# A fused attention and expert kernel: the first batch's turned z gets the layout of the later ones

## The chip, the cores and the metric

The kernel runs on one core of one Trainium2 chip. Its time is the device time of one execution in microseconds (us). The core has four compute engines that the text names: TensorE (PE in the rows; its weight loads are PEld), VectorE (DVE), ScalarE (ACT) and GpSimd (POOL). SyncE (SP) and GpSimd issue the DMAs. Each engine works through its own instructions in order; semaphores tie the engines together.

## The reference

Two layers follow each other. The first is an attention without softmax over 8 batches of 2816 tokens, with keys and queries both z (64 wide) and values v (256 wide):

```
scores = z @ z.T / 2816
attn   = relu(scores) ** 2
x      = u * (attn @ v)
```

The second is a mixture of experts on all 22528 rows of x: a dense part, relu(x @ w1_dense) @ w2_dense, plus, for the one of 8 experts that has the largest logit of x @ w_gate, the softmax weight of that expert times relu(x @ w1[e]) @ w2[e].

## The kernel before, in words

A batch is cut into 22 blocks of 128 tokens. z is turned so that its 64 columns lie on partitions; as they fill only half of the 128, two copies are kept, one on partitions 0 to 63 and one on 64 to 127, and TensorE runs two 64-row matmuls beside each other, one on either half. For the batches after the first the turn is a DMA transpose (`turn_z`, line 127), which takes two blocks at a time and so leaves block k on the lower half and block k + 1 on the upper; `cross_z` (line 136) then copies the blocks to the other half, crossed, into the odd places. For the first batch, whose z comes in three DMAs, TensorE makes the turn itself (`turn_z0`, line 227): each block is turned twice, once into either half, in four parts, and every part is copied out of PSUM by ScalarE or VectorE (line 233). The function `swapped` tells by batch which layout holds.

The scores are symmetric: a block of A = relu(.)**2 for queries i and keys k is the transpose of that for queries k and keys i. So groups of 2, 4, 4, 4, 4 and 4 query blocks (`groups`) compute only the key rows that no earlier group has; `far_steps` brings the others by DMA transposes on SP's queue (line 557), into spare places of the weight tile or of the tile `zn` (`slots`, `mirror`). `scores` (line 466) makes a tile s of 1024 columns in one of four pairs of PSUM banks (`pairs`); `relu` takes it to SBUF (`first`, lines 482 and 484) and squares it into A (`second`, lines 498 and 500). `av` runs the output matmuls of two query blocks at a time (line 698): 22 key blocks with each half of the array on one of the two outputs, then, after a change of rows, 22 more with the halves exchanged. At the change (`swap_rows`), TensorE must not have the two halves write the same output; so either one touch (`touch`, line 635, a matmul into a PSUM pair of its own) and two tiles of scores stand between (a filled change), or two touches (a plain change, also used where the logits of the expert stage have to go in).

The order of all this is made at build time by a planner written in Python. `now` is its clock of TensorE, `free` its clocks of the other engines. Work for ScalarE, VectorE and GpSimd is put in a list with `offer(ready, rank, ways, then)`, where `ways` gives for each engine a planned duration; `best` takes what can start earliest, the lower rank first among equals, and refuses an engine that would end later than another one would, by more than a margin:

```
                if len(ways) > 1:
                    end = min(at[x] + ways[x][0] for x in ways if x != eng)
                    if t + dur > end + (0.0 if rank in (0.9, 4) else 0.6):
                        continue
```

`fill` places scores between output matmuls while PSUM pairs are free by these clocks; `need` lets the planner's TensorE wait for blocks of A. `at` and `soon` tie further work to ticks, two for every pair of query blocks: `small_constants` (from line 257) writes, at tick 7 and in one piece, eight small tables that the routing of the expert stage uses much later, without the planner's clock of VectorE being moved.

After the attention, from about 540 us, the expert stage runs: for each tile of tokens two matmul layers of the dense part and of one expert (lines 1107 and 1118), with ScalarE and VectorE taking the results out and GpSimd scattering the rows to the output.

Of the kernel before, what the change touches and what calls it, by code (L numbers as in the profile page):

```python
# [12 lines left out]
ALU = mybir.AluOpType  # L13
AX = mybir.AxisListType
ET = mybir.EngineType
P = 128
# [3 lines left out]
def kernel(  # L20
# [12 lines left out]
    nc = tc.nc  # L33
# [6 lines left out]
    nK = S // P  # L40
# [79 lines left out]
    def swapped(b, x):  # L120
        return x % 2 if b else 0
# [10 lines left out]
    def cross_z(b, h):  # L132

        x = zT_of[b][:].rearrange("p (k h) t -> p k h t", h=2)
        mine, other = slice(h * dq, (h + 1) * dq), slice((1 - h) * dq, (2 - h) * dq)
        nc.vector.tensor_copy(x[mine, :, 1, :], x[other, :, 0, :])
        if h == 1:
            z_there.add(b)
# [76 lines left out]
    parts0 = [(0, Z1), (Z1, Z2), (Z2, 16), (16, nK)]  # L215
    z0_cast = [0.25, 1.7, 2.5, 2.5]
    z0_left = list(range(len(parts0)))
    z0_turned = {}

    def turn_z0(n):  # L220
        k0, k1 = parts0[n]
        until(lambda: pairs[0][0] if pairs else None)
        x = take_pair()
        zp = banks(x, "zp", (P, 2, 8, P), BF)[:, 0]
        for k in range(k0, k1):
            for h in range(2):
                nc.tensor.transpose(out=zp[h * dq:(h + 1) * dq, k - k0, :],
                                    in_=z_of[0][:, k, :], identity=ident[:])
        now[0] = max(now[0], z0_cast[n]) + 0.05 + 0.13 * (k1 - k0)
        c = (k1 - k0) * P  # L230

        def copy(eng):
            (nc.scalar.copy if eng == "act" else nc.vector.tensor_copy)(
                zT_of[0][:, k0:k1, :], zp[:, :k1 - k0, :])

        def there(t):
            z0_turned[n] = t + 0.15
            give_pair(t + 0.1, x)

        offer(now[0] + 0.2, -1, {"act": (0.2 + c / 1280, copy), "dve": (0.16 + c / 1960, copy)}, there)  # L240

    te = const.tile([P, E], I32, name="te")
# [5 lines left out]
    free.update(act=1.0, dve=0.3, pool=2.4)  # L248
# [7 lines left out]
    def small_constants():  # L256
        nc.vector.memset(wg[:, 0, 0:1], 0.0)
        nc.gpsimd.dma_start(out=wg[:], in_=moe_w_gate.rearrange("(c p) e -> p c e", p=P))
        nc.gpsimd.affine_select(out=ntri[:], in_=ntri[:], compare_op=ALU.is_ge,
                                fill=0.0, base=0, pattern=[[-1, P]],  # L260
                                channel_multiplier=1)
        nc.vector.tensor_copy(desc8[:], ti[:])
        nc.vector.tensor_copy(ecap[:], te[:])
        nc.vector.tensor_copy(base[:], te[:])
        nc.vector.tensor_copy(sf[:], it[:])
        nc.vector.tensor_scalar(out=it0[:], in0=sf[:, 0:NH], scalar1=float(P), scalar2=None,
                                op0=ALU.mult)
        nc.vector.tensor_scalar(out=it1[:], in0=sf[:], scalar1=float(T2), scalar2=float(T2 - 1),
                                op0=ALU.mult, op1=ALU.add)
        nc.vector.tensor_copy(pjf[:], pj[:])  # L270
        nc.vector.memset(one8[:], 1.0)
# [44 lines left out]
    def best():  # L316
        pick = None
        for op in todo:
            rank, num, ready, ways, then = op
            at = {x: max(free[x], ready) for x in ways}  # L320
            if "pool" in ways:

                at["pool"] = max(at["pool"], both["dve"])
            for eng, (dur, fn) in ways.items():
                t = at[eng]
                if len(ways) > 1:

                    end = min(at[x] + ways[x][0] for x in ways if x != eng)
                    if t + dur > end + (0.0 if rank in (0.9, 4) else 0.6):
                        continue  # L330
                if rank == 1:
                    if not r_free:
                        continue
                    t = max(t, r_free[0])
                key = (t, rank, num)
                if pick is None or key < pick[0]:
                    pick = (key, op, eng)
        return pick
# [39 lines left out]
    def slots(b):  # L378

        return (list(mirror) if b < B - 1 else []) + ([(1, 5)] if 0 < b < B - 1 else [])  # L380
# [68 lines left out]
    def scores(n, ks, x=None):  # L449
# [5 lines left out]
        if n == 0:  # L455
# [3 lines left out]
            until(lambda: max(z0_turned[x] for x in mine) if set(mine) <= set(z0_turned) else None)  # L459
            until(lambda: pairs[0][0] if pairs else None)  # L460
        sx = take_pair() if x is None else x
        s = banks(sx, "s")
        for y, k in enumerate(ks):
            for h in range(2):
                r = slice(h * dq, (h + 1) * dq)
                nc.tensor.matmul(out=s[:, h, y * c:(y + 1) * c],  # L466
                                 lhsT=zT[r, k + h - swapped(b, h), :],
# [3 lines left out]
        relu(n, ks, s, c, now[0] + (0.3 if n == 0 else 0.2), sx)  # L471
        run(now[0])

    def relu(n, ks, s, c, ready, sx):
# [36 lines left out]
        def half(t):  # L511
            give_pair(t + 0.1, sx)
            more = 0.08 if n < 3 else 0.0
            ways = {"act": (0.12 + more + c / 600, second), "dve": (0.08 + more + c / 480, second)}
            if n < 3:

                ways = {"act": (0.2 + c / 600, second), "pool": (0.15 + c / 290, second)}
            offer(t + 0.15, 4 if n > 2 else 0.9, ways, done)

        more = 0.06 if n < 3 else 0.0  # L520
# [18 lines left out]
    def block(n, k, c):  # L539

        b, _, w = groups[n]
        for a in far[n]:
            _, j0, wj = groups[a]
            if j0 <= k < j0 + wj:
                x = c * wj + (k - j0 ^ swapped(b, c))
                return turned_to(a, n, w)[:, x * P:(x + 1) * P]
        c ^= swapped(b, k)
# [91 lines left out]
    def swap_rows(n):  # L639

        keep[0] = 0
        if at_swap or ahead(n) is None or n == 0 and not (len(pairs) > 1 and pairs[1][0] <= now[0]):
# [576 lines left out]
    at(7, small_constants)  # L1219
# [203 lines left out]
```

## Time and profile before

| | us |
|---|---|
| median of 3 runs | 861.49 (860.99 to 862.01) |
| the profiled execution | 861.74 |
| its span, first to last instruction | 860.0 |

| engine | busy us | share of the span |
|---|---|---|
| TensorE | 847.5 | 99% |
| TensorE weight loads | 760.5 | 88% |
| ScalarE | 686.9 | 80% |
| VectorE | 643.0 | 75% |
| GpSimd | 495.3 | 58% |

In the table a share is busy time over the whole span; in the attention stage ScalarE and VectorE are fuller than in the expert stage. A matmul's busy time includes its way through the array, which overlaps the next one's, so TensorE's pace is read from the starts of its instructions rather than from their lengths. In rows of a timeline the first number is the start, the second the time from the first start to the last end of the merged instructions, "x8" their count, and in square brackets stands the idle time of the engine before them and what ended it.

### The profile page before, as it was taken

The numbers are of one execution on the slowest core, as the hardware profiler recorded it, in microseconds if no ns is written. First come the engines' busy times: TensorE is split into PE (matmuls) and PEld (weight loads), VectorE is DVE, ScalarE is ACT, GpSimd is POOL, SyncE is SP. The second block draws the span as 40 slices with busy tenths as digits, with TensorE's granted clock in tenths as the row PEclk, the third lists the DMA queues.
The fourth block names the chain that finished last, engine by engine and source line by source line (L and its number), as shares of the span: only waits on it lengthen the run. The fifth ranks groups of instructions, "written<-read, shape, count | busy, mean of one in ns | idle before, by whom it ended". The sixth has DMA issues, their size and how long they took to land. (4 is left out here: it accounts for less than half of the span.)

```text
span 860.0 us, 30273 instructions
## 1 busy us (share of the span) xinstructions
PE 847.5 (99%) x12238; PEld 760.5 (88%) x12238; DVE 643.0 (75%) x1096; ACT 686.9 (80%) x857; POOL 495.3 (58%) x612
## 2 busy tenths in 40 slices
PE   8999999999999999999999999999999999999997
PEld 7998898898898899899899888888888888889996
DVE  6999978988988988988988994756554444445664
ACT  8999978977987987987987994677777777777775
POOL 6404456357346557446546567777767655555565
PEclk9999999999999999999999999999999999999999
DMA  7989999999999989989999787765544544444332
GB/s 161 179 173 175 188 164 182 219 169 185 207 179 191 209 176 193 208 178 178 199 190 173 143 167 126 123 139 133 132 113 125 121 118 114 114 109 103 92 97 87
DMA packets 279086, 134.00 MB, mean 156 GB/s; under 512 B 247710, under 2 KB 255006, under 8 KB 278944
## 3 DMA queue, kind: packets, MB, share of 16 engines
q1 hardware_dynamic: 252240, 76.42, 51.5%
q0 software_dynamic: 26704, 55.64, 30.0%
q8 instruction: 96, 1.57, 0.8%
q14 instruction: 46, 0.38, 0.2%
HBM read 61.53 MB, written 37.03 MB: 115 GB/s over the span
## 5 line engine op out<-in xcount | busy, mean ns | idle before, releaser
L698 PE MATMUL o<-vb,A 64*128 64x256 bf16 x6992 | 444.2, 269 | 0.0
L698 PEld LDWEIGHTS <-A 64*128 64x128 bf16 x6992 | 371.4, 94 | 32.1 <-issue 0.7
L868 POOL DMA_INDIRECT xs<-pays,pi x176 | 188.9, 1074 | 167.9 <-issue 60.3
L482 ACT ACTIVATE r<-s 128x1024 f32<-128x1024 f32 (+1 forms) x230 | 227.4, 1007 | 41.6 <-PE s L466 22.7
L1112 ACT ACTIVATE ring<-h_ps 128x1024 bf16<-128x1024 f32 x180 | 183.1, 1018 | 87.7 <-PE h_ps L1107 85.6
L498 ACT ACTIVATE A<-r 128x1024 bf16<-128x1024 f32 (+1 forms) x246 | 247.0, 1031 | 2.2 <-DVE r L484 0.9
L484 DVE TENSOR_SCALAR r<-s 128x1024 f32<-128x1024 f32 (+1 forms) x156 | 187.4, 1215 | 6.1 <-PE s L466 4.3
L1132 POOL DMA_INDIRECT out_dram<-ring,me x140 | 143.7, 1026 | 79.0 <-PE yy L1118 41.4
L1147 DVE SCALAR_TENSOR_TENSOR ring<-yy,me,ring 128x256 f32<-128x256 f32 x179 | 86.3, 483 | 132.0 <-ACT ring L1146 126.2
L500 DVE TENSOR_TENSOR A<-r 128x1024 bf16<-128x1024 f32 x134 | 162.1, 1227 | 2.6 <-DMA A<-A 1.0
L1118 PEld LDWEIGHTS <-ring 128*128 128x128 bf16 x1432 | 139.3, 98 | 15.7
L466 PE MATMUL s<-zT 64*128 64x512 bf16 (+1 forms) x908 | 141.5, 344 | 2.7 <-DVE r L484 1.4
L1118 PE MATMUL yy<-ring,ring 128*128 128x256 bf16 x716 | 107.4, 273 | 0.0
L1118 PE MATMUL yy<-w2d,ring 128*128 128x256 bf16 x716 | 107.4, 273 | 0.0
L1107 PE MATMUL h_ps<-ring,w1d 128*128 128x256 bf16 x720 | 92.9, 272 | 0.0
L727 DVE TENSOR_TENSOR pays<-o,ut 128x512 bf16<-128x512 f32 x88 | 60.3, 686 | 32.6 <-POOL pays L866 17.6
L1107 PE MATMUL h_ps<-ring,ring 128*128 128x256 bf16 (+1 forms) x784 | 84.2, 253 | 0.0
L1081 DVE COPY ring<-wall 128x2048 bf16 x109 | 74.5, 699 | 9.9 <-DVE ring L1147 4.2
L1107 PEld LDWEIGHTS <-ring 128*128 128x128 bf16 x872 | 73.8, 98 | 7.0 <-DVE ring L1081 0.2
L866 POOL COPY pays<-gt 128x2 f32<-128x2 f32 x176 | 69.2, 393 | 15.1 <-DMA xs<-pays,pi 10.8
L1107 PEld LDWEIGHTS <-w1d 128*128 128x128 bf16 x720 | 69.8, 98 | 8.2 <-issue 0.2
L466 PEld LDWEIGHTS <-zT 64*128 64x128 bf16 x908 | 54.5, 94 | 14.2 <-issue 3.6
(125 smaller groups left out, 461.7 us busy)
## 6 DMA issues: line engine op xcount, KB each, us to landing
ut<-in_u_dram SPq DMA_DIRECT2D x88, 256.0 KB
vb<-in_v_dram POOLq DMA_DIRECT2D x14, 448.0 KB
wall<-in_moe_w_dram POOLq DMA_DIRECT2D x16, 256.0 KB
vb<-in_v_dram POOLq DMA_DIRECT2D x7, 512.0 KB
xs<-pays,pi POOLq DMA_INDIRECT x176
zr<-in_z_dram POOLq DMA_DIRECT2D x7, 352.0 KB
out_dram<-ring,me POOLq DMA_INDIRECT x140
ring<-xs SPq DMA_TRANSPOSE x109
```

The costliest lines, as they stand in the source:

```text
L466: nc.tensor.matmul(out=s[:, h, y * c:(y + 1) * c], lhsT=zT[r, k + h - swapped(b, h), :], rhs=zT[r, i0:i0 + w, :], start=True, stop=True)
L482: nc.scalar.activation(r[:, :, :c], s[:, :, :c], AF.Relu, scale=1.0 / S)
L484: nc.vector.tensor_scalar(out=r[:, :, :c], in0=s[:, :, :c], scalar1=1.0 / S, scalar2=0.0, op0=ALU.mult, op1=ALU.max)
L498: nc.scalar.activation(a, r, AF.Square)
L500: (nc.gpsimd if eng == "pool" else nc.vector).tensor_mul(a, r, r)
L698: last_av[0] = nc.tensor.matmul(out=o[:, j, 0:D], lhsT=block(n, k, i + j - i0)[r], rhs=v_of[b][r, k, :], start=(nth == 0 and x == 0), stop ...
L868: ins = behind(lambda: nc.gpsimd.indirect_dma_start(out=xs, out_offset=bass.IndirectOffsetOnAxis(ap=rs[q][:, j:j + 1], axis=0), in_=row(g) ...
L1107: ins = nc.tensor.matmul(out=h_ps[:, f, hs, :], lhsT=w1(c, f), rhs=xT[:, hs, c, :], start=(c == 0), stop=(c == 1)).ins
L1112: nc.scalar.activation(h[:, :, 0:m * P], h_ps[:, :, 0:m, :].rearrange("p f h t -> p f (h t)"), AF.Relu)
L1118: ins = nc.tensor.matmul(out=y[:, k, :], lhsT=h[:, f, j * P:(j + 1) * P], rhs=w2(f), start=(f == 0), stop=(f == 3))
L1132: ins = behind(lambda: nc.gpsimd.indirect_dma_start(out=out, out_offset=bass.IndirectOffsetOnAxis(ap=ix, axis=0), in_=ys, in_offset=None, ...
L1147: nc.vector.scalar_tensor_tensor(out=ys, in0=y[:, 1, :], scalar=me[:, j, 0:1], in1=yd, op0=ALU.mult, op1=ALU.add)
```

## The change

`swapped` no longer looks at the batch: in all batches block k is on the lower half at place k, and the block beside it on the upper. `turn_z0` turns two blocks with one 128x128 transpose into the even places, in three parts (blocks 0 to 3, 4 to 9, 10 to 21); only place 1, which group 0 needs as queries, is made by two turns of one block. When the last scores of group 0 have been placed, `cross_z0` offers four VectorE copies that make the other odd places; scores of later groups wait for them in the planner. The margin of rank -1 (the copies out of PSUM) becomes 0. The small constants begin at tick 5, and their eight VectorE operations are offered one by one at ticks 4 to 11. The first batch, too, gets the slot (1, 5). Squares of group 3 go to ScalarE or GpSimd, as those of groups 0 to 2 did. And `swap_rows` takes the plain way for any group when the second PSUM pair isn't free by the planner's clock; until now it did so for group 0 alone, and otherwise waited for the pair.

```diff
-    def swapped(b, x):
-        return x % 2 if b else 0
+    def swapped(x):
+        return x % 2
...
-    def cross_z(b, h):
+    def cross_z(b, h, k0=0, k1=nK // 2):
-        x = zT_of[b][:].rearrange("p (k h) t -> p k h t", h=2)
+        x = zT_of[b][:].rearrange("p (k h) t -> p k h t", h=2)[:, k0:k1]
...
-    parts0 = [(0, Z1), (Z1, Z2), (Z2, 16), (16, nK)]
-    z0_cast = [0.25, 1.7, 2.5, 2.5]
+    parts0 = [(0, Z1), (Z1, Z2), (Z2, nK)]
+    z0_cast = [0.25, 1.35, 2.55]
...
-        for k in range(k0, k1):
-            for h in range(2):
-                nc.tensor.transpose(out=zp[h * dq:(h + 1) * dq, k - k0, :],
-                                    in_=z_of[0][:, k, :], identity=ident[:])
-        now[0] = max(now[0], z0_cast[n]) + 0.05 + 0.13 * (k1 - k0)
-        c = (k1 - k0) * P
+        m = (k1 - k0) // 2 + (n == 0)
+
+        def turn(j, k, w, h):
+            nc.tensor.transpose(out=zp[h:h + w * dq, j, :], in_=z_of[0][:, k:k + w, :].rearrange("p k d -> p (k d)"),
+                                identity=ident[:])
+
+        js = [j for j in range(m) if n or j != 1]
+        for j, k in zip(js, range(k0, k1, 2)):
+            turn(j, k, 2, 0)
+        if n == 0:
+            turn(1, 1, 1, 0)
+            turn(1, 0, 1, dq)
+        now[0] = max(now[0], z0_cast[n]) + 0.05 + 0.065 * (m + (n == 0))
+        c = m * P
...
+    def cross_z0():
+        for x, k0, k1 in ((0, 1, Z2 // 2), (1, Z2 // 2, nK // 2)):
+            for h in range(2):
+                offer(now[0], 0, {"dve": (0.1 + (k1 - k0) * 0.05,
+                                          lambda eng, h=h, k0=k0, k1=k1: cross_z(0, h, k0, k1))},
+                      lambda t, x=x: crossed.__setitem__(x, t + 0.15))
...
-                    if t + dur > end + (0.0 if rank in (0.9, 4) else 0.6):
+                    if t + dur > end + (0.0 if rank in (-1, 0.9, 4) else 0.6):
...
-        return (list(mirror) if b < B - 1 else []) + ([(1, 5)] if 0 < b < B - 1 else [])
+        return (list(mirror) if b < B - 1 else []) + ([(1, 5)] if b < B - 1 else [])
...
+        elif b == 0:
+            until(lambda: crossed.get(min(n - 1, 2) // 2))
+        if b == 0:
             until(lambda: pairs[0][0] if pairs else None)
...
-                                 lhsT=zT[r, k + h - swapped(b, h), :],
+                                 lhsT=zT[r, k, :],
...
+        if n == 0 and not left[0]:
+            cross_z0()
...
-            more = 0.08 if n < 3 else 0.0
+            more = 0.08 if n < 4 else 0.0
             ways = {"act": (0.12 + more + c / 600, second), "dve": (0.08 + more + c / 480, second)}
-            if n < 3:
+            if n < 4:
                 ways = {"act": (0.2 + c / 600, second), "pool": (0.15 + c / 290, second)}
-            offer(t + 0.15, 4 if n > 2 else 0.9, ways, done)
+            offer(t + 0.15, 4 if n > 3 else 0.9, ways, done)
...
-        if at_swap or ahead(n) is None or n == 0 and not (len(pairs) > 1 and pairs[1][0] <= now[0]):
+        if at_swap or ahead(n) is None or not (len(pairs) > 1 and pairs[1][0] <= now[0]):
...
-    at(7, small_constants)
+    at(5, small_constants)
+    for x, fn in enumerate(tables):
+        soon(4 + x, fn, 0.2)
```

The list `tables` holds the eight operations that stood in `small_constants`.

## Rows read from the trace of the kernel before

**Rows 1.** The page: the engines' busy time, share of the span and instructions; and the clock granted to TensorE in 40 slices of the span, in tenths.

```profile
PE 847.5 (99%) x12238; PEld 760.5 (88%) x12238; DVE 643.0 (75%) x1096; ACT 686.9 (80%) x857; POOL 495.3 (58%) x612
...
PEclk9999999999999999999999999999999999999999
```

**Rows 2.** What TensorE waited for over the whole run, longest first: us in total, times, longest.

```profile
PE lg L761 <- DMA ring<-xs: 1.4, 1, 1.4
PE s L466 <- DVE r L484: 1.4, 2, 1.0
```

**Rows 3.** The timeline of TensorE's matmuls from the start to 12.7 us.

```profile
1.22 2.10 PE L207 MATMUL warm<-ones 128*128 128x128 bf16 x18 [1.22 <-DVE ones L201]
...
3.47 0.64 PE L227 MATMUL zp<-ident,zr 128*64 128x128 bf16 x8
4.85 0.61 PE L466 MATMUL s<-zT 64*128 64x256 bf16 x4 [0.74 <-ACT zT L233]
5.39 2.13 PE L227 MATMUL zp<-ident,zr 128*64 128x128 bf16 x36
7.46 1.04 PE L466 MATMUL s<-zT 64*128 64x256 bf16 x8
8.28 1.06 PE L698 MATMUL o<-vb,A 64*128 64x256 bf16 x8
9.13 0.90 PE L466 MATMUL s<-zT 64*128 64x256 bf16 x10
11.03 0.29 PE L466 MATMUL s<-zT 64*128 64x256 bf16 x2 [0.99 <-DVE r L484]
11.14 1.27 PE L698 MATMUL o<-vb,A 64*128 64x256 bf16 x20
...
12.67 0.17 PE L635 MATMUL d<-ones 64*128 64x8 bf16 x1
```

**Rows 4.** The timeline of ScalarE from 3 to 14 us.

```profile
4.22 0.58 ACT L233 COPY zT<-zp 128x512 bf16<-128x512 bf16 x1
5.50 1.02 ACT L482 ACTIVATE r<-s 128x1024 f32<-128x1024 f32 x1 [0.71 <-PE s L466]
6.56 1.15 ACT L498 ACTIVATE A<-r 128x512 bf16<-128x512 f32 x2
```

**Rows 5.** The timeline of VectorE from 3 to 14 us.

```profile
6.28 1.20 DVE L233 COPY zT<-zp 128x768 bf16<-128x768 bf16 x2 [3.00 <-PE zp L227]
8.11 1.22 DVE L484 TENSOR_SCALAR r<-s 128x1024 f32<-128x1024 f32 x1 [0.63 <-PE s L466]
9.76 2.95 DVE L484 TENSOR_SCALAR r<-s 128x1024 f32<-128x1024 f32 x3 [0.43 <-PE s L466]
```

**Rows 6.** The timeline of GpSimd from 9 to 20 us.

```profile
9.64 4.19 POOL L500 TENSOR_TENSOR A<-r 128x512 bf16<-128x512 f32 x4 [4.50 <-ACT r L482]
```

**Rows 7.** Groups of instructions by line and form in 0 to 60 us: busy us, mean ns of one, idle before.

```profile
L136 DVE COPY zT<-zT 64x1408 bf16<-64x1408 bf16 x2 | 1.1, 554 | 0.1
```

**Rows 8.** Busy time of each engine (and its instructions) in stretches of the run; the stretch and its length first, at the end granted clock, DMA share and GB/s.

```profile
12.00:38.00 26.00, 25.91 (x476) 25.13 (x473) 23.71 (x34) 24.72 (x27) 17.01 (x16) 1.00 0.94 181
...
45.40:82.00 36.60, 36.60 (x630) 32.87 (x627) 36.01 (x54) 35.15 (x39) 7.47 (x11) 1.00 0.94 165
```

The engines stand in the order PE, PEld, DVE, ACT, POOL.

**Rows 9.** The timeline of TensorE's matmuls around 54 us: one item of scores with 512 columns, and what follows it.

```profile
53.73 0.40 PE L466 MATMUL s<-zT 64*128 64x512 bf16 x2
53.95 0.40 PE L698 MATMUL o<-vb,A 64*128 64x256 bf16 x4
```

**Rows 10.** The timeline of SP's queue from 27 to 39 us.

```profile
27.44 3.17 SPq L557 DMA_TRANSPOSE A<-A  x1
...
32.99 1.67 SPq L729 DMA_TRANSPOSE xT<-pays  x1
38.87 0.33 SPq L181 DMA_DIRECT2D ut<-in_u_dram  x1
```

**Rows 11.** The timeline of VectorE from 37.2 to 39 us: the first of the small constants, and the gating multiply (line 727) behind them.

```profile
37.28 0.20 DVE L262 CAST desc<-ti 128x88 f32<-128x88 int32 x1
...
38.17 0.68 DVE L727 TENSOR_TENSOR pays<-o,ut 128x512 bf16<-128x512 f32 x1
```

**Rows 12.** The timeline of TensorE's matmuls, short pieces around the touches from 26 to 51 us.

```profile
26.08 0.17 PE L635 MATMUL d<-ones 64*128 64x8 bf16 x1
26.10 0.65 PE L466 MATMUL s<-zT 64*128 64x256 bf16 x8
...
32.28 0.17 PE L635 MATMUL d<-ones 64*128 64x8 bf16 x1
...
38.90 0.16 PE L635 MATMUL d<-ones 64*128 64x8 bf16 x1 [0.28 <-DVE pays L727]
...
45.35 0.17 PE L635 MATMUL d<-ones 64*128 64x8 bf16 x1
...
51.28 0.17 PE L635 MATMUL d<-ones 64*128 64x8 bf16 x1
```

**Rows 13.** The same view around a plain change, and around a filled one near the end of the attention stage.

```profile
16.03 0.43 PE L635 MATMUL d<-ones 64*128 64x8 bf16 x2
16.31 0.39 PE L698 MATMUL o<-vb,A 64*128 64x256 bf16 x4
...
512.29 0.61 PE L466 MATMUL s<-zT 64*128 64x512 bf16 x4 [0.34 <-DVE pays L727]
```

More of the change, by code (lines that the diff above doesn't have):

```diff
@@ L214 @@
     nc.scalar.copy(z_of[0][:, Z1:Z2, :], z0[:, Z1:Z2, :])
-    parts0 = [(0, Z1), (Z1, Z2), (Z2, 16), (16, nK)]
-    z0_cast = [0.25, 1.7, 2.5, 2.5]
+    parts0 = [(0, Z1), (Z1, Z2), (Z2, nK)]
+    z0_cast = [0.25, 1.35, 2.55]
     z0_left = list(range(len(parts0)))
     z0_turned = {}
+    crossed = {}
     def turn_z0(n):
@@ L224, in turn_z0 @@
         zp = banks(x, "zp", (P, 2, 8, P), BF)[:, 0]
-        for k in range(k0, k1):
-            for h in range(2):
-                nc.tensor.transpose(out=zp[h * dq:(h + 1) * dq, k - k0, :],
-                                    in_=z_of[0][:, k, :], identity=ident[:])
-        now[0] = max(now[0], z0_cast[n]) + 0.05 + 0.13 * (k1 - k0)
-        c = (k1 - k0) * P
+        m = (k1 - k0) // 2 + (n == 0)
[10 more added lines that the diff above has]
+        c = m * P
         def copy(eng):
-            (nc.scalar.copy if eng == "act" else nc.vector.tensor_copy)(
-                zT_of[0][:, k0:k1, :], zp[:, :k1 - k0, :])
+            to = zT_of[0][:, 0:m, :]
+            if n:
+                to = zT_of[0][:].rearrange("p (k h) t -> p k h t", h=2)[:, k0 // 2:k1 // 2, 0, :]
+            (nc.scalar.copy if eng == "act" else nc.vector.tensor_copy)(to, zp[:, :m, :])
         def there(t):
@@ L247 @@
     nc.gpsimd.iota(pj[:], pattern=[[0, 1]], base=0, channel_multiplier=1)
-    free.update(act=1.0, dve=0.3, pool=2.4)
+    free.update(act=1.3, dve=0.3, pool=2.4)
     sf = const.tile([P, N // T2], F32, name="sf")
@@ L261, in small_constants @@
                                 channel_multiplier=1)
[L262 to L271, printed above, removed]
+    tables = [
+        lambda: nc.vector.tensor_copy(desc8[:], ti[:]),
+        lambda: nc.vector.tensor_copy(sf[:], it[:]),
+        lambda: nc.vector.tensor_copy(ecap[:], te[:]),
+        lambda: nc.vector.tensor_copy(base[:], te[:]),
+        lambda: nc.vector.tensor_scalar(out=it0[:], in0=sf[:, 0:NH], scalar1=float(P), scalar2=None,
+                                        op0=ALU.mult),
+        lambda: nc.vector.tensor_scalar(out=it1[:], in0=sf[:], scalar1=float(T2),
+                                        scalar2=float(T2 - 1), op0=ALU.mult, op1=ALU.add),
+        lambda: nc.vector.tensor_copy(pjf[:], pj[:]),
+        lambda: nc.vector.memset(one8[:], 1.0)]
     zero = []
@@ L512, in half @@
             give_pair(t + 0.1, sx)
-            more = 0.08 if n < 3 else 0.0
+            more = 0.08 if n < 4 else 0.0
             ways = {"act": (0.12 + more + c / 600, second), "dve": (0.08 + more + c / 480, second)}
-            if n < 3:
+            if n < 4:
                 ways = {"act": (0.2 + c / 600, second), "pool": (0.15 + c / 290, second)}
-            offer(t + 0.15, 4 if n > 2 else 0.9, ways, done)
-        more = 0.06 if n < 3 else 0.0
+            offer(t + 0.15, 4 if n > 3 else 0.9, ways, done)
+        more = 0.06 if n < 4 else 0.0
         ways = {"act": (0.12 + more + c / 600, first), "dve": (0.1 + more + c / 480, first)}
@@ L544, in block @@
             if j0 <= k < j0 + wj:
-                x = c * wj + (k - j0 ^ swapped(b, c))
+                x = c * wj + (k - j0 ^ swapped(c))
                 return turned_to(a, n, w)[:, x * P:(x + 1) * P]
-        c ^= swapped(b, k)
+        c ^= swapped(k)
         return keys(n, k, k + 1)[:, 0, c * P:(c + 1) * P]
```

## The prediction

> **What bounds the kernel now.** I read the page first: TensorE is busy 99% of the span [rows 1]. Then the waits of TensorE over the whole run: the two largest are 1.4 us each, of them one ahead of the late logits and two waits of scores for VectorE's ReLU, and the others smaller [rows 2]. All but the first lie in the first 43 us or at changes of rows. So the rest of the run is a fixed stream of matmuls, and only three kinds of time can change: the start-up, the stalls named there, and the number of matmuls. The start-up is where most is lost. Its timeline [rows 3] shows z turned from 3.47, one group of scores at 4.85, 36 more turns, scores at 7.46, eight output matmuls at 8.28, ten of the scores at 9.13, and then 0.99 us idle up to 11.03; from 11.03 the stream is dense. The timelines of ScalarE, VectorE and GpSimd [rows 4 to 6] show who keeps it waiting. Times of the trace are of one execution of 861.74 us (860.0 of it span); the median of the runs shown is 861.49, 0.25 us lower, so I apply the sum of changes to the median.
>
> **The start-up.** Before, 44 turns of one block each (8 from 3.47, 36 from 5.39 for 2.13 us); after, 13 turns, 11 of them of two blocks at once. One 128x128 turn is a 128-column matmul; 18 such warm matmuls take 2.10 us with the last one's 0.31 of pipeline, about 0.105 each [rows 3]. I go through it with these prices, the planner's costs deciding only who does what.
> 1. First part: four turns instead of eight begin at 3.47 as before and end near 4.05. The copy out of PSUM goes to VectorE, since the margin of 0.6 for rank -1 is gone; 384 columns there are half of the 0.56 us for 768 (two take 1.20 with their gap, [rows 5]), about 0.3 with a fixed part, so 4.1 to 4.4. Before, ScalarE took it and ended at 4.80 (4.22 + 0.58) [rows 4]. First scores at 4.45 instead of 4.85, first ReLU at 5.1 instead of 5.50: 0.4 us won.
> 2. Second part: three turns from 4.95 to 5.5, copy to 5.85, scores at 5.9 instead of 7.46, ReLU on ScalarE at 6.55 instead of VectorE at 8.11: 1.5 us won.
> 3. Third part: it now stands behind those scores. Six turns from 6.45 to 7.3, copy 0.56 to 7.9, scores at 7.95; before, the third scores left at about 7.86. Nothing is won, because copy, scores and turns now follow one another where before all 36 turns ran in one piece. The ReLU of it is on VectorE, 8.6 to 9.8.
> 4. The other scores of group 0 go at 8.4 to 9.4 (before, from 9.13). All four PSUM pairs are then full, so the first output matmul waits for VectorE at 9.8; before it ran at 8.28, but TensorE then stood from 10.03 on.
> 5. New on VectorE: four copies that make the crossed places, 64 x 512 twice and 64 x 768 twice. 64 x 1408 takes 0.554 [rows 7], so by size 0.2 + 0.2 + 0.3 + 0.3 = 1.0 us. They stand behind the ReLU that ends at 9.8 and before the next one, which starts at 10.9; in the kernel before, VectorE's last full ReLU of that group began at about 10.98 (9.76 + 1.22). The time that the halved PSUM copies save is paid out here. Group 1's scores wait for the first two of them (10.2), and for PSUM longer.
> 6. The first change of rows needs blocks 0 to 15 of A. The ReLU of blocks 12 to 15 is on ScalarE at 9.2 to 10.2; the squares then take two halves of 0.57 on ScalarE (to 11.4, [rows 4]) and two of 1.04 on GpSimd (to 12.4, [rows 6]). So that change comes at 12.5 to 12.8; before it was at 12.67 [rows 3].
>
> I take 0.0 for the start-up. The bounds: the idle stretch before 11.03 won, -1.0; or the four copies wholly on the path, +1.0.
>
> **Fewer scores in batch 0.** With (1, 5) among its slots, group 5 of the first batch takes group 1's blocks by a DMA transpose, and the rows k = 2 and 4 of its scores go: two items of two 512-column matmuls. One such item holds TensorE from 53.73 to 53.95, 0.22 us [rows 9], so -0.44 (bounds -0.44 and 0, if the space becomes a wait). ReLU and square of 128x1024 go with each, 1.0 to 1.2 us each, four operations in all, which matters in 45 to 82 us, where VectorE is busy 36.0 of 36.6 us [rows 8]. The added transpose stands on SP's queue, where those of group 1 take 3.2 us; behind it wait the next u load and the xT transposes, and SP is free from 34.7 to 38.9 [rows 10], so it costs nothing; without that cover, late u would stop the gating multiply and with it PSUM.
>
> **Small constants.** At 37.28 eight small VectorE operations stand in a row, to 38.2; the gating multiply comes after them, and TensorE's touch at 38.90 waits for it [rows 11, 12]. Between touches, the stretch with that wait takes 6.62 us and the one before, with as many matmuls, 6.20; the next takes 6.45 and the one behind it, of its own content, 5.93 [rows 12]. So the row and its after-effect (the second wait of rows 2 for VectorE's ReLU lies there) cost 0.42 + 0.52 = 0.94. After the change each operation is offered by itself at ticks 4 to 11 with a planned cost of 0.2, so no wait of theirs passes 0.3. The same 1 us of VectorE has still to be paid while it is busy 23.7 of 26 us [rows 8]; squares of group 3 leave VectorE for GpSimd (17.0 of 26 busy) in exchange. I take -0.8 (bounds -0.94 and 0).
>
> **Plain changes of rows.** A filled change costs almost nothing: touch at 26.08, scores at 26.10. A plain one has two touches, 16.03 to 16.31 [rows 12, 13], so each further plain one costs 0.25 and puts its scores elsewhere. The condition now also takes the plain way for later groups when the second pair isn't free by the planner's clock. Rows of before show scores or touches late twice between 38 and 45 us [rows 2, 12]; I take one to two more plain changes, +0.3 (bounds 0 and eight changes of the first batch, +2.0). The late wait at 512.29 (0.34 idle, [rows 13]) and a like one are of this kind too; but scores went in there as if PSUM had been free, and a test by the same clock doesn't see the real delay: 0 (bound -0.35).
>
> **Sum.** 0.0 - 0.44 - 0.8 + 0.3 = -0.9, so 861.5 - 0.9 = 860.6 us. Ends of the single bounds: -1.0 - 0.44 - 0.94 - 0.35 = -2.7, and +1.0 + 2.0 = +3.0.
>
> **Rivals.**
> *A, the start-up gains.* If the four copies hide and steps 1 and 2 carry through, the idle 1.0 us goes: -1.0 - 0.44 - 0.94 + 0.3 = -2.1, 859.4 us. For it: the second scores come 1.5 us sooner. Against: steps 3 and 4.
> *B, the stalls only move.* VectorE and ScalarE are full until 82 us, so spread constants and crossed copies could come back as other waits, and plain changes eat the saved scores: 0.0, 861.5 us. For it: 24.7 and 23.7 of 26 us busy in 12 to 38 us [rows 8]. Against: TensorE has no wait there now.
> *C, TensorE runs longer at half rate, slower than before.* The granted clock of the page is full from the first slice [rows 1], but the pace says otherwise: 8 output matmuls take 1.06 us at 8.28, and 20 take 1.27 at 11.14 [rows 3]; they run in pairs, and taking off the last one's length (0.42 and 0.27, from the ends of these rows) that is 0.64 over three steps and 1.00 over nine, 0.21 and 0.11 a pair: the first is the level of 1.2 GHz, the other that of 2.4. The rise came near 9.4, after 4 us in which TensorE hardly paused (5.39 to 9.4). After the change it turns a third as many blocks and pauses near 5.5, 7.5, 9.5. If the rise comes only once the stream has been dense again, at about 16 us, then some 6 us from 9.9 on run at half rate and lose 3.0: -0.9 + 3.0 = +2.1, 863.6 us. It decides from a rise 1.8 us of dense work later than 9.4, where its 0.9 eats the gain.
> The Trainium skill, page "TensorE: Matmul & The Clock Gate", section "Part 1: The HAM clock gate", says the slow state is the default and that activity of TensorE is what ends it; the pace in rows 3 agrees, and no row here shows what a start with holes does. By that rule the change, which takes early activity away, would speak for C.
>
> **How the numbers follow.** Chances: forecast 0.45, A 0.20, B 0.20, C 0.15. About 0.2% (1.7 us) is what a measurement of this kernel can tell from no change. The forecast falls beyond -1.7 one time in ten (0.045) and beyond +1.7 hardly; A is beyond 7 in 8 (0.17); B stays within, one in ten on either side (0.02 each); C is beyond 3 in 4 (0.11). With the forecast's own misses, faster 0.24, slower 0.13, same 0.63. The range from 858.9 to 863.1 holds the forecast, A, B, and the half of C with an earlier rise; the forecast's own is 859.9 to 861.4.
>
> **What would show it.** The first score matmul at 4.45 and the second at 5.9; the first output matmul near 9.9; the first touch at 12.5 to 12.8 (A: under 11.8; C: beyond 13.3 with pairs of output matmuls 0.21 apart). Touches some 6.2 us apart, none 6.6, up to 45 us. Two fewer 512-column score pairs in batch 0. One or two more pairs of touches before 80 us. The prediction is wrong if the touches behind 82 us stand apart by other than before, or if the distance from the last touch to the end changes by over 0.5 us.

## The result and the profile after

The change made the kernel slower. Its median is 871.01 us (865.17 to 886.93, 21 executions) beside 861.64 us for the kernel before (860.85 to 872.04, 21 executions on the same chip). The ratio is 1.0057, with a 95% interval of 1.0032 to 1.0083; the forecast was 860.6 us. Some executions of either kernel are held up by DMAs behind 200 us, by other amounts each time (in the first profile after, a transpose of z that starts at 213.69 on SP's queue takes 9.45 us, in the profile before 1.97), so the ratio leaves the most disturbed ones out. I compare by two numbers that this hardly touches. The first is the lowest time: 864.60 us in 22 executions of the kernel after, with the experiment e10 below, against 860.31 us in all executions of the kernel before, +4.3; in the 21 of each alone it is 865.17 against 860.85, +4.3 too. The second is the start of the second group of logits, a place near 100 us that every kernel here passes and behind which little differs (at most two tiles of scores, 0.22 us each, and one change of rows).

The first fence is the page of the profiled execution after (880.87 us; span 879.1), the rows that answer to [rows 1].

```profile
PE 855.1 (97%) x12208; PEld 758.7 (86%) x12208; DVE 642.5 (73%) x1096; ACT 685.8 (78%) x853; POOL 496.9 (57%) x615
```

TensorE runs 30 instructions fewer: 31 turns and four score matmuls went, five touches came (117 instead of 112). It is busy 7.6 us longer all the same; the parts of the run at a slower pace, shown below, add to that (e10, with fewer of them, is busy 848.6).

For the reading by time I use the second profile of the same kernel, e10, which took 864.60 us (span 862.9). Its waits of TensorE over the whole run, longest first (us in total, times, longest), answer to [rows 2]:

```profile
PE o L725 <- POOL A L527: 2.0, 1, 2.0
PE s L491 <- DVE zT L247: 1.2, 3, 0.5
PE warm L207 <- DVE ones L201: 1.2, 1, 1.2
PE s L491 <- DVE ut L179: 1.2, 1, 1.2
```

Two of these are new: an output matmul that waits 2.0 us for a square on GpSimd, and scores that wait 1.2 us for VectorE. (The 1.2 for `ones` is the warm-up; three short waits for the turned z are what a copy of each of the three parts costs.) Both new ones lie in the timeline of TensorE's matmuls in e10, answering to [rows 3] and [rows 12]:

```profile
3.47 0.62 PE L231 MATMUL zp<-ident,zr 128*128 128x128 bf16 x4
4.55 0.61 PE L491 MATMUL s<-zT 64*128 64x256 bf16 x4 [0.46 <-DVE zT L247]
...
6.04 0.61 PE L491 MATMUL s<-zT 64*128 64x256 bf16 x4 [0.45 <-DVE zT L247]
...
8.06 1.46 PE L491 MATMUL s<-zT 64*128 64x256 bf16 x12 [0.33 <-DVE zT L247]
9.77 2.52 PE L725 MATMUL o<-vb,A 64*128 64x256 bf16 x24 [0.25 <-DVE r L511]
...
12.67 0.17 PE L662 MATMUL d<-ones 64*128 64x8 bf16 x1
14.00 0.61 PE L491 MATMUL s<-zT 64*128 64x256 bf16 x8 [1.16 <-DVE ut L179]
...
39.62 1.27 PE L725 MATMUL o<-vb,A 64*128 64x256 bf16 x20
42.86 0.61 PE L725 MATMUL o<-vb,A 64*128 64x256 bf16 x8 [1.97 <-POOL A L527]
43.31 0.42 PE L662 MATMUL d<-ones 64*128 64x8 bf16 x2
```

Up to the first output matmul the start is the forecast's, nearly to the tenth. Then 24 output matmuls take 2.52 us, where 20 took 1.27 before [rows 3]; and the scores that should fill the change of rows at 12.67 come only at 14.00, after 1.16 us of idle time. At 42.86 the stream breaks, and the touch behind it is a pair, a plain change.

The second logits start at 98.45 us in e10 and at 94.20 before: +4.25; from there to the eleventh group of logits e10 takes 297.34 us and the kernel before 297.35. (The two spans stand only 2.9 us apart, because the profile before has a wait of 1.4 us for a DMA at 541.69 [rows 2] that e10 does not have.) I account for the 4.25 by touches. Each pair of 256-column matmuls is taken at its full pace of 0.109 us, each turn and warm-up matmul at half of that (two turns beside each other count once), and the rest is called lost. Up to the touch at 21.96 (20.14 before) 10.1 us are lost instead of 7.5: +2.6. Four more pairs of touches up to 50 us at 0.25: +1.0. The stretch from 34.79 to 43.31 takes 8.52 us, 2.6 above its matmuls; the two disturbed stretches of [rows 12] lost 1.05: +1.6. Other stretches give 0.2 back, and there is 0.7 us less work in front of the logits, 0.5 of it turns. 2.6 + 1.0 + 1.6 - 0.2 - 0.7 = 4.3.

**The pace of the start.** The first profile of the kernel after shows it further on than e10:

```profile
9.77 2.74 PE L725 MATMUL o<-vb,A 64*128 64x256 bf16 x24 [0.26 <-DVE r L511]
...
12.49 1.09 PE L725 MATMUL o<-vb,A 64*128 64x256 bf16 x8
13.35 0.21 PE L662 MATMUL d<-ones 64*128 64x8 bf16 x1
14.00 0.61 PE L491 MATMUL s<-zT 64*128 64x256 bf16 x8 [0.42 <-DVE ut L179]
```

Eight output matmuls take 1.09 us here, the 1.06 of [rows 3] at 8.28, which is the pace of 1.2 GHz; single pairs start 0.21 apart up to 13.13. In e10 they do so up to 11.86 (the eight at 12.23 take 0.61), in the kernel before up to 9.35. The page shows the full clock here too, as it did there [rows 1], because it counts as full all time ahead of the trace's first clock record. In each trace that first record, at full clock, begins just where the starts draw together: at 9.53 us before, at 11.93 in e10 and at 13.72 in the first profile. Over all 13 profiles it begins at 8.22 to 10.35 in the four with the old start (the kernel before, e6, e7, e8) and at 11.56 to 14.44 in the nine with the new one, so the new start makes the rise later in every one of them. What TensorE did before is different: 13 turns and gaps of 0.46, 0.45 and 0.33 us instead of 44 turns and one gap of 0.74 [rows 3]. By the first touch e10 has lost 0.8 us more than the kernel before and the first profile 1.5 more (7.95 and 8.63 us, 7.17 before). Yet in both the scores come at 14.00.

**Why the scores at 14.00 are late.** VectorE in e10, as [rows 5] before:

```profile
8.50 1.23 DVE L511 TENSOR_SCALAR r<-s 128x1024 f32<-128x1024 f32 x1 [0.49 <-PE s L491]
9.75 2.94 DVE L136 COPY zT<-zT 64x512 bf16<-64x512 bf16 x4
12.73 1.85 DVE L511 TENSOR_SCALAR r<-s 128x1024 f32<-128x1024 f32 x2
```

The four crossed copies take 2.94 us, where I had 1.0, and the next ReLU starts at 12.73 instead of 10.9. GpSimd, in the first profile of the kernel after, runs two squares over nearly the same time (and a third one later that matters below); behind it are VectorE's groups by form in 8 to 14 us, with the mean ns of one copy:

```profile
10.03 2.08 POOL L527 TENSOR_TENSOR A<-r 128x512 bf16<-128x512 f32 x2 [1.44 <-ACT r L509]
...
27.26 1.90 POOL L527 TENSOR_TENSOR A<-r 128x1024 bf16<-128x1024 f32 x1 [1.58 <-ACT r L509]
```

```profile
L136 DVE COPY zT<-zT 64x768 bf16<-64x768 bf16 x2 | 1.4, 718 | 0.0
L136 DVE COPY zT<-zT 64x512 bf16<-64x512 bf16 x2 | 1.4, 716 | 0.1
```

Both forms have one mean of 0.72 although one is half as large again: the copies are not slow by their size. Taken singly they last 0.29, 1.14, 1.08 and 0.35; the long two are as long as a square on GpSimd (1.04). Two of the small constants show it more plainly. The first two rows are VectorE's, the third is GpSimd's:

```profile
28.15 1.06 DVE L284 CAST desc<-ti 128x88 f32<-128x88 int32 x1
...
40.99 1.85 DVE L287 CAST base<-te 128x8 f32<-128x8 int32 x1
```

```profile
40.90 1.90 POOL L527 TENSOR_TENSOR A<-r 128x1024 bf16<-128x1024 f32 x1
```

The cast to `base`, 8 numbers a partition, took 0.16 us before:

```profile
37.47 0.16 DVE L264 CAST base<-te 128x8 f32<-128x8 int32 x1
```

Now it takes 1.85 and ends at 42.84, beside a square that ends at 42.80; the one at 28.15 took 0.20 before [rows 11] and now ends at 29.21, beside the square from 27.26 to 29.16. ReLUs, which read PSUM, don't show it: before, three ran in 2.95 beside GpSimd's squares [rows 5, 6]. So an operation of VectorE that reads and writes SBUF seems to wait until a square on GpSimd ends. The Trainium skill, page "SBUF — State Buffer", section "SBUF: two separate sides", says that GpSimd and some operations of VectorE (those in a two-port mode, or with two inputs in SBUF beside a GpSimd operation that reads SBUF) share a pair of ports, which the first to start holds for its whole instruction while the other is blocked. The rows agree that the second one is blocked (1.85 us for a cast of 0.16); which mode a copy or cast runs in they don't show. The experiment e9 below tests the hold.

**Why TensorE stops at 42.86.** GpSimd in e10:

```profile
34.72 1.88 POOL L527 TENSOR_TENSOR A<-r 128x1024 bf16<-128x1024 f32 x1 [0.55 <-DVE r L511]
36.56 4.32 POOL L302 DMA_DIRECT2D xs<-zero  x8
40.90 1.90 POOL L527 TENSOR_TENSOR A<-r 128x1024 bf16<-128x1024 f32 x1
```

Eight DMAs that zero parts of `xs` stand on GpSimd's queue in one piece, 0.54 us each, and the square that TensorE needs starts only behind them, with no idle time in between. `zero_fill` has no lines in the diff; it is tied to ticks, and the planner does not move GpSimd's clock for it. The kernel before has the same eight, but a square falls between them:

```profile
32.66 1.68 POOL L280 DMA_DIRECT2D xs<-zero  x3 [2.41 <-DVE zero L279]
34.33 1.92 POOL L500 TENSOR_TENSOR A<-r 128x1024 bf16<-128x1024 f32 x1
36.17 2.71 POOL L280 DMA_DIRECT2D xs<-zero  x5
```

**The pace behind it.** In the first profile the same wait, of 1.98 us, had a sequel that e10 doesn't show. TensorE's matmuls of the first profile, and then two windows (after the stretch and its length: busy us of PE, PEld, DVE, ACT and POOL, and the granted clock first of the three numbers at the end), the first profile's and e10's:

```profile
42.86 0.61 PE L725 MATMUL o<-vb,A 64*128 64x256 bf16 x8 [1.98 <-POOL A L527]
...
45.32 2.93 PE L725 MATMUL o<-vb,A 64*128 64x256 bf16 x28
```

```profile
44.00:48.00 4.00, 4.00 (x48) 2.90 (x46) 2.45 (x2) 3.80 (x4) 3.72 (x2) 0.57 1.04 237
```

```profile
44.00:48.00 4.00, 4.00 (x76) 3.41 (x74) 3.43 (x3) 3.75 (x4) 3.72 (x2) 1.00 1.22 151
```

28 output matmuls take 2.93 us where 28 took 1.69 at 35.67 in the same profile. The granted clock is 0.57 over these 4 us, so most of them are at 1.2 GHz, and 48 matmuls run where e10 has 76. It costs 1.7 us: the second logits are at 100.11 in that profile.

### The profile page after: what moved, and what is told of

It reads as the page before. It is cut to its first block, busy times and chain, and to the rows that moved or that the text cites. A ratio compares the mean times of both kernels' runs of the same rounds, so it can differ in the third digit from the quotient of the medians.

```text
span 879.1 us, 30213 instructions
## 1 busy us (share of the span) xinstructions
PE 855.1 (97%) x12208; PEld 758.7 (86%) x12208; DVE 642.5 (73%) x1096; ACT 685.8 (78%) x853; POOL 496.9 (57%) x615
## 4 chain that ended last, share of the span: by engine, by line
PE 86%; DMA 7%; POOL 2%; issue 2%; DVE 1%; ACT 1%; SPq 0%; POOLq 0%; DVEq 0%; ACTq 0%
PE o L725 42%; PE h_ps L1134 17%; PE yy L1145 17%; PE s L491 9%; DMA wall<-A 3%; DMA vb<-in_v_dram 1%; POOL out_dram L1159 1%; PE lg L788 1%; DMA A<-A 1%; DMA me<-xs 1%; DVE r L511 1%; ACT r L509 1%; ACT A L525 0%; DMA xs<-pays,pi 0%; POOL A L527 0%
## 5 line engine op out<-in xcount | busy, mean ns | idle before, releaser
L509 ACT ACTIVATE r<-s 128x1024 f32<-128x1024 f32 x228 | 226.1, 1007 | 47.7 <-PE s L491 29.7
L511 DVE TENSOR_SCALAR r<-s 128x1024 f32<-128x1024 f32 x156 | 187.9, 1216 | 17.7 <-PE s L491 14.7
L527 DVE TENSOR_TENSOR A<-r 128x1024 bf16<-128x1024 f32 x129 | 155.2, 1219 | 8.9 <-DMA A<-A 6.9
L1108 DVE COPY ring<-wall 128x2048 bf16 x109 | 74.5, 698 | 10.1 <-DMA wall<-in_moe_w_dram 4.2
L893 POOL COPY pays<-gt 128x2 f32<-128x2 f32 x176 | 64.9, 369 | 28.6 <-DMA xs<-pays,pi 24.1
```

What stands on the lines that cost most here:

```text
L509: nc.scalar.activation(r[:, :, :c], s[:, :, :c], AF.Relu, scale=1.0 / S)
L511: nc.vector.tensor_scalar(out=r[:, :, :c], in0=s[:, :, :c], scalar1=1.0 / S, scalar2=0.0, op0=ALU.mult, op1=ALU.max)
L527: (nc.gpsimd if eng == "pool" else nc.vector).tensor_mul(a, r, r)
```

## The experiments

I began with two theories. The first: the wait for GpSimd comes from the squares of group 3 that the change gives it, with the zero fills in front. The rival: the plain changes put the scores elsewhere, and so everything behind them.

**e1, squares back.** The kernel after with the squares of group 3 as before:

```diff
-            if n < 4:
+            if n < 3:
```

(and `n > 2`, and the additions `more` to the planned durations of squares and ReLUs, as before).

> The changed kernel with group 3's squares as before (ScalarE or VectorE). Theory 1: in the changed kernel a square of group 3 stands on GpSimd behind eight zero fills (4.32 us of issuing, 36.56 to 40.88), TensorE waits 1.98 us for it at 42.86 and then runs some 3 us at half rate: both go, 2.0 + 1.7 = 3.7 us less than the changed kernel. Rival (the plain changes and the full VectorE make the loss): under 1 us less, and another wait of TensorE of over 1 us before 60 us.

Measured: 872.76 us, ratio 1.006 (1.0007 to 1.0113); second logits at 99.77. The wait stays, and with it the slow pace (granted clock 0.58 in 44 to 48 us):

```profile
42.85 0.61 PE L725 MATMUL o<-vb,A 64*128 64x256 bf16 x8 [2.43 <-POOL A L527]
```

GpSimd's eight DMAs at 36.56 and the square at 40.89 stand as they did. That part of the first theory falls: the square that TensorE waits for is there without the edit for group 3, so it belongs to an earlier group, and the edit is not the cause.

**e2, the old rule for changes of rows.**

```diff
-        if at_swap or ahead(n) is None or not (len(pairs) > 1 and pairs[1][0] <= now[0]):
+        if at_swap or ahead(n) is None or n == 0 and not (len(pairs) > 1 and pairs[1][0] <= now[0]):
```

> The changed kernel with the old rule for plain changes (group 0 alone). Theory 2: five more plain changes in the first batch cost 0.24 us each, so 1.2 us less than the changed kernel, and the wait at 42.9 stays. Rival: filled changes have to wait for PSUM there, nothing is won or some is lost.

Measured: 870.15 us, ratio 1.0067 (1.0024 to 1.011); second logits at 98.84, touches 112 again. The wait for GpSimd is gone, though the eight DMAs are still in one piece (39.23 to 43.56, no needed square behind them). Four waits for VectorE's ReLU came instead, 3.0 us in all up to 95 us:

```profile
PE s L491 <- DVE r L511: 3.0, 4, 1.1
PE s L491 <- DVE ut L179: 1.3, 1, 1.3
```

So the rival holds: nothing is won over e10's 98.45. The new rule does what it says, it avoids waits for PSUM; by itself it is not where the time went.

**e4, both back** (e1 and e2 together).

> Both undone: squares of group 3 and the rule for plain changes as before. If theories 1 and 2 add up: 4.9 us less than the changed kernel, so about the time of the kernel before; what is left over it is the start-up (first touch 13.35 against 12.67, and 0.65 of wait behind it). Rival (the loss is the disturbed stretches behind 200 us): it stays 3 us or more over the kernel before.

Measured: 871.67 us, ratio 1.0053 (1.0006 to 1.0099); its lowest execution, the profiled one, took 863.88. Second logits at 96.80, 2.6 us later than before. Left are the wait at 14.00 (1.25) and two for the ReLU at 35.34 (0.40) and 40.47 (1.02), where the kernel before has 1.4 in two [rows 2]. The theories don't add up to 4.9: e4 is 1.65 us ahead of e10 and 3.3 ahead of the first profile. Of the 2.6 us left the start makes 2.0 (the touch at 21.96 instead of 20.14, with 0.2 us less done by then); the stretch with the two waits, from 34.06 to 42.00, loses 0.8 more than the two disturbed stretches of [rows 12].

**e3 and e11, zero fills on SP.** The kernel after with the DMAs on another queue, run twice:

```diff
-        nc.gpsimd.dma_start(out=xs[e * CAP:e * CAP + P, :], in_=zero[0][:])
+        nc.sync.dma_start(out=xs[e * CAP:e * CAP + P, :], in_=zero[0][:])
```

> The changed kernel with the eight zero fills issued by SP instead of GpSimd. Theory 1 (place in GpSimd's queue): the square starts by 39 us, the wait of 1.98 us and the half rate behind it go, 3.7 us less. Rival (a square on GpSimd takes 1.9 us and is late in any case): a wait of over 1 us stays there, under 1.5 us less.

> The kernel after the change with the eight zero fills on SP's queue once more. The first time its second logits were 3.8 us earlier and its end was not. Theory 'the late loss was a disturbance': second logits at 96.2 to 96.4, the wait near 550 us (3.6 us, for VectorE's small operations) is gone or smaller, and the lowest time is 2 to 4 us under that of the kernel after, 861.5 to 863.5. Rival 'zero fills on SP put something else late': the same wait near 550 us in this profile, and no time under 866.

Measured at the place in question, in e3: no wait and no slow pace, the touch at 41.14 instead of 43.30, second logits at 96.30, 3.8 us earlier than in the first profile of the kernel after and 2.15 earlier than in e10. The rows of TensorE:

```profile
39.62 1.71 PE L725 MATMUL o<-vb,A 64*128 64x256 bf16 x28
41.14 0.43 PE L662 MATMUL d<-ones 64*128 64x8 bf16 x2
...
42.74 1.69 PE L725 MATMUL o<-vb,A 64*128 64x256 bf16 x28
```

This shows what the zero fills cost: 2.15 us for the wait, and 1.7 more in executions where the pace falls after it. Yet the time got worse, 877.54 us (ratio 1.013, 1.0056 to 1.0205) and 884.34 (1.0194, 1.0083 to 1.0305), and of ten executions none is under 874. Both profiles have this wait near 550 us, and no other one here has the first layer of the experts wait over 1.2 us (e11's row):

```profile
PE h_ps L1134 <- DVE inc L854: 3.4, 1, 3.4
```

My expectation that the late loss was a disturbance is wrong; the rival holds, zero fills on SP put something late. The traces lead one step further. In VectorE's queue a copy of expert weights (L1108) stands in front of the small operations, and it waits for the DMA that brings the weights; e11's row, then e10's:

```profile
558.03 0.69 DVE L1108 COPY ring<-wall 128x2048 bf16 x1 [6.51 <-DMA wall<-in_moe_w_dram]
```

```profile
541.60 0.69 DVE L1108 COPY ring<-wall 128x2048 bf16 x1 [3.05 <-DMA wall<-in_moe_w_dram]
```

GpSimd issues the last DMA of these weights 6.6 us behind the 16th group of logits in e11 and 6.7 in e3, in the other eleven profiles 2.1 to 3.4. Why GpSimd comes to it late, and why more of the stretches behind 200 us are held up, stays open. (e11's second logits are at 98.39, not 96.3; one wait of 1.25 us at 84.95, for a DMA of v, makes most of that.)

**e9, no GpSimd beside the copies.** The kernel after; group 0's squares never go to GpSimd:

```diff
-            if n < 4:
+            if 0 < n < 4:
```

> The kernel after the change, but group 0's squares (the first group's) go to VectorE or ScalarE, never to GpSimd, so that GpSimd computes nothing while the crossed copies run. This is a look at one duration, not at the time: the planner deals out the first 14 us anew. Theory 'the copies are held by GpSimd': the four crossed copies of VectorE take 0.29 to 0.36 us each, some 1.2 to 1.4 us in all, wherever they land. Rival 'a copy that crosses partitions is slow by itself': two of the four, or all, stay at 0.7 to 1.1 us each. If the first theory holds but the ReLUs and squares now crowd VectorE and ScalarE, the first touch can still be as late as 13.3; the durations decide, not the touch.

GpSimd computes nothing from 5.1 to 15.2 us. VectorE's copies there:

```profile
12.86 0.29 DVE L136 COPY zT<-zT 64x512 bf16<-64x512 bf16 x1
...
13.20 0.29 DVE L136 COPY zT<-zT 64x512 bf16<-64x512 bf16 x1
...
13.65 0.36 DVE L136 COPY zT<-zT 64x768 bf16<-64x768 bf16 x1
...
14.04 0.35 DVE L136 COPY zT<-zT 64x768 bf16<-64x768 bf16 x1
```

They take 1.29 us for the four, as the first theory had it; crossing partitions is not slow by itself. The start gains nothing, since the squares now crowd VectorE and ScalarE and the copies start at 12.86 instead of 9.75: second logits at 98.36, 865.83 us.

**e5, the copies on ScalarE** (e4, and for the first batch:)

```diff
-    def cross_z(b, h, k0=0, k1=nK // 2):
+    def cross_z(b, h, k0=0, k1=nK // 2, eng="dve"):
...
-        nc.vector.tensor_copy(x[mine, :, 1, :], x[other, :, 0, :])
+        (nc.scalar.copy if eng == "act" else nc.vector.tensor_copy)(x[mine, :, 1, :], x[other, :, 0, :])
...
-                offer(now[0], 0, {"dve": (0.1 + (k1 - k0) * 0.05,
-                                          lambda eng, h=h, k0=k0, k1=k1: cross_z(0, h, k0, k1))},
+                offer(now[0], 0, {"act": (0.2 + (k1 - k0) * 0.1,
+                                          lambda eng, h=h, k0=k0, k1=k1: cross_z(0, h, k0, k1, eng))},
```

> e4 with the four crossed copies of the first batch on ScalarE. Theory 3: on VectorE they take 2.94 us instead of the 1.0 forecast, two of them held for as long as a square runs on GpSimd (1.14 and 1.08 against 0.29), and so the next ReLU starts at 12.7 and the scores at 14.00 after 1.25 us of wait. On ScalarE no copy is as long as GpSimd's square, VectorE's ReLU starts by 10.5, the wait of 1.25 falls under 0.5, and the second logits come at 95.5 to 96.0 (e4: 96.80, kernel before: 94.20). Rival (ScalarE is as full as VectorE, the squares behind the copies come later): first touch after 13.3, second logits at 96.8 or later.

Second logits at 95.59, 1.2 us earlier than in e4, and the wait of 1.25 is gone:

```profile
9.77 2.74 PE L725 MATMUL o<-vb,A 64*128 64x256 bf16 x24 [0.25 <-DVE r L511]
...
13.33 0.17 PE L662 MATMUL d<-ones 64*128 64x8 bf16 x1
13.33 0.65 PE L491 MATMUL s<-zT 64*128 64x256 bf16 x8
```

The scores follow the touch at once, but that comes at 13.33, after the slow pace. From there to the touch at 21.02 no more is lost than in the kernel before, so 1.4 us of the start's loss are there without the hold, lost by the first touch and mostly to the pace, and the copies on VectorE add 1.2. (e5 takes the copies off VectorE, not only the hold. That the hold alone makes the wait is worked out from lengths: 1.65 of the 2.94 us are hold, more than the wait of 1.25.) In e10, where the pace rises sooner than in the first profile, the wait for VectorE is longer by as much: both lead to 14.00. The time, 881.08 us in two executions (1.0193, 1.0114 to 1.0272), is ruled by DMA waits far behind and tells nothing of this edit.

**e6, e7 and e8: single gains on the kernel before.** e6 adds only the spread constants (the first diff, with the list `tables`), e7 only the slot (the second), and e8 both.

```diff
-    at(7, small_constants)
+    at(5, small_constants)
+    for x, fn in enumerate(tables):
+        soon(4 + x, fn, 0.2)
```

```diff
-        return (list(mirror) if b < B - 1 else []) + ([(1, 5)] if 0 < b < B - 1 else [])
+        return (list(mirror) if b < B - 1 else []) + ([(1, 5)] if b < B - 1 else [])
```

> The kernel before with the small constants spread alone. Forecast's term: the stretches between touches from 32 to 45 us lose their 0.94, second logits at 93.3 (before 94.20). Rival (VectorE is full there and the new order makes other waits): 94.0 or later, with waits for VectorE's ReLU elsewhere before 60 us.

> The kernel before with the slot (1, 5) in the first batch alone. Forecast's term: two items of 512 columns fewer, 0.44 us, second logits at 93.76. Rival (the added DMA transpose delays others, or the space becomes a wait): 94.2 or later.

> The kernel before with both, constants spread and slot (1, 5), the start-up, the squares and the rule for plain changes left alone. If the two terms add up: second logits at 92.9 and the undisturbed end 1.3 us under the kernel before, faster than both kernels. If they don't: 94 or later.

| | median us | ratio (95%) | second logits |
|---|---|---|---|
| e6 | 865.54 | 1.0007 (0.9969 to 1.0045) | 94.39 |
| e7 | 865.26 | 1.0002 (0.9964 to 1.004) | 94.05 |
| e8 | 865.07 | 1.0004 (0.9963 to 1.0045) | 94.31 |

The kernel before had a median of 865.27 in that series. None can be told from it by its time. At the third logits, by which all scores of the first batch are done, the kernel before stands at 129.46, e6 at 129.87, e7 at 129.31 and e8 at 129.36. In e6 the wait for the row of constants is gone, but others came up to 95 us, where the kernel before had 1.4 in two for the ReLU and 0.3 for `pays`:

```profile
PE s L468 <- DVE r L486: 0.9, 2, 0.6
...
PE s L468 <- DVE wg L257: 0.6, 1, 0.6
```

These runs also tell what moves the zero fills together. They stand in one piece in e1, e2, e4 and e5, but in two, with a square between them, in e6, e7 and e8, which have the old start, and in e9, whose start is planned otherwise. So it is the new start with its order, and not the spread constants, the slot, the squares of group 3 or the rule for changes of rows.

**e10, the kernel after once more.**

> The kernel after the change once more, for a profile that may be less disturbed behind 200 us. Theory 'all that the change does lies ahead of 100 us': the second logits start at 99.8 to 100.4 again, the touches up to there stand within 0.1 us of those of the first profile, and in stretches without a DMA wait the distance from there to the end is that of the kernel before. Rival 'the change also loses time later': some stretch behind 100 us is longer than before in both profiles of this kernel.

The second logits came at 98.45, 1.35 us under my lower bound, since the pace did not fall at 45 us; the touches up to 43 us stand as in the first profile, save the first (12.67 instead of 13.35). Behind 100 us the distances between groups of logits are those of the kernel before within 0.02 us up to 530 us; from there to the end e10 takes 1.3 us less, as it lacks the wait of 1.4. So the cost lies ahead of 100 us, and whether the kernel after is also held up more often than the one before (the medians stand 9.4 us apart, the lowest times 4.3) stays open.

No version here beats the kernel before.

## Why the prediction was wrong

The prediction was wrong in its mechanism, not only in its number: a start held up by GpSimd and by a late rise of the pace, a wait in GpSimd's queue and more plain changes cost 4.3 us where it expected to win 0.9.

**Start-up, forecast 0.0, measured about +2** (2.6 lost, less some 0.5 for the fewer turns). Steps 1 to 4 hold: the scores at 4.45, 5.9 and 7.95 came at 4.55, 6.04 and 8.06, the first output matmul at 9.77 instead of 9.9. Step 5 failed, by the size of its term: four copies at 1.0 us took 2.94, because I took their price from a row where GpSimd did not compute beside them [rows 7], while my own step 6 had two of its squares end at 12.4, right there. e9 shows the hold (1.29 us without GpSimd beside them), e5 what the copies on VectorE cost, 1.2 us. Step 6 failed by the pace: a touch at 12.5 to 12.8 was e10's 12.67, but 13.35 and 13.33 in the first profile and in e5. My sign for rival C, a touch beyond 13.3 with pairs 0.21 apart, was met in these two and not in e10; how late the pace rises differs from one execution to the next (11.93 and 13.72). The bound of +1.0, "the four copies wholly on the path", assumed their undisturbed length and the pace of before.

**Fewer scores, forecast -0.44.** Of the right sign, its size not settled: at the third logits e7 stands 0.15 us ahead of the kernel before, and e8 0.51 ahead of e6.

**Small constants, forecast -0.8, measured 0 to +0.4** (at the third logits e6 stands 0.41 us behind the kernel before, and e8 0.05 behind e7). That VectorE's 1 us "has still to be paid" stood in the step, and I priced it at next to nothing. Rival B was right on this term.

**Plain changes, forecast +0.3 for one or two, measured +1.2 for five.** The price of 0.25 each is right [rows 13]; the count was a guess from two late places, inside the bound of eight. e2 shows what the rule buys: without it there are 3.0 us of waits for the ReLU.

**Not in the sum at all: GpSimd's queue, +2.2, or +3.8 with the slow pace.** I counted the queue of SP for the added transpose and left out GpSimd's, though the change moves squares and ticks there. Rows of the kernel before show the zero fills, split 3 and 5 around a square; I did not ask what stands in front of each square once the split moves. e3 shows that the wait and its sequel go with them.

**The rivals.** A fell: the copies were not hidden. B holds for the constants alone. C, given 0.15, named a mechanism that is there: the pace rises at 11.6 to 14.4 us instead of 8.2 to 10.4, with 0.8 us more lost by the first touch in e10 and 1.5 in the first profile, not the 3.0 I gave it, and in both that lies under the hold of VectorE, as the scores come at 14.00 either way. That the new start is the cause the clock records of all profiles show; whether it is the fewer turns or the gaps between them is not shown, as no run filled the gaps with other matmuls. The second fall of the pace, at 45 us, came in two of three profiles whose TensorE had stood for 2.0 to 2.4 us (the first and e1), and not in e10 after 1.97. C's 863.6 us comes close to the lowest time by luck, as most of the loss is not the pace's. The range's upper end of 863.1 missed even the lowest time, by 1.5 us.

## What to carry to other kernels

When a change gives VectorE a copy inside SBUF, look up what GpSimd computes in those microseconds, and take the copy's price from a row with the same company. Where a planner does not book DMA issues on an engine's clock, any edit that shifts its order can put a needed operation behind a whole row of them; so list what stands in front of the critical operations on every queue, also of code without a line in the diff. And what a sparser start does to TensorE's pace belongs into the sum, by the starts of the first dense matmuls.

## What the hardware showed

The length of a small VectorE operation can be set wholly by GpSimd: 8 numbers a partition in 1.85 us instead of 0.16. A square on VectorE, with its input in SBUF, is held too; in the kernel before, this one takes 2.28 us where the next takes 1.21, beside GpSimd's square from 34.33 to 36.25:

```profile
35.07 2.28 DVE L500 TENSOR_TENSOR A<-r 128x1024 bf16<-128x1024 f32 x1
```

And an idle TensorE of about 2 us may or may not be followed by some 3 us at the lower clock: one kernel, the same wait (1.98 and 1.97 us), granted clock 0.57 in one execution and 1.00 in the other. Nor does one program always reach the full clock at the same time: 11.93 us in one profile of the kernel after and 13.72 in the other.
